# Where the two causal masks of a tile stand beside the scans, and the order of TensorE's two products

## The chip, the cores and the metric

The kernel runs on one core of one Trainium2 chip. The metric is the device time of one execution in microseconds (us). TensorE (PE, with its weight loads as PEld), VectorE (DVE), ScalarE (ACT), GpSimd (POOL) and the DMA queues work side by side, each through its own instructions in program order, and wait for one another only through semaphores.

## The reference, cut to what matters

```python
# attention: B, H, S, D = 4, 8, 768, 48; state is D x D for each head
for t in range(S):
    state = alpha[:, :, t, :, None] * state + k_t (outer) v_t
    y[:, :, t] = q_t @ state
# y as [3072, 384] tokens, then
x = gate_w * (relu(x @ w1[e]) @ w2[e])      # the expert e with the largest logit, 8 experts, 1024 wide
out = square(relu(x @ w_in)) @ w_out        # 2048 wide
```

The recurrence is computed in chunks of 128 steps. With a chunk's running product of alpha folded into q (qt) and the running product from the other end into k (kt), the output of a chunk is a masked product (qt by kt, causal, times v) plus a cross product (qt times the state at the chunk's start), and the state moves on by kt times v.

## The kernel before, in words

There are 24 tiles of 128 tokens, six to a sequence. The attention takes roughly the first 154 us; expert layers and the last feed-forward layer follow.

`prep(n)` is VectorE's work for a tile, five instructions: the forward scan `acum` (L460), a small reciprocal, the backward scan `rs` (L464), and the two products `qt` (L466) and `kt` (L468). `qk_mm(n)` multiplies kt by qt on TensorE into two PSUM tiles `sp` (L488, j = 0 and 1), ScalarE copies each to SBUF (L491), and GpSimd's `affine_select` (L477) sets what lies above the diagonal to zero; the result is `pm`. `k_T(n)` transposes kt (L499) and ScalarE copies it (L501). `kv_mm(n)` forms the new state in PSUM (L511, L515) and VectorE writes it as `sd` (L518). `y_mm(n)` gathers in one PSUM tile `y` the masked product (L529) and, where the tile is not the first of its sequence, the cross product with the state (L532); ScalarE copies it out (L534).

The order on every engine is that of the code. Step n of the main loop issues `qk_mm(n + 1)`, `k_T(n + 1)`, `kv_mm(n)`, `prep(n + 3)`, `y_mm(n)`, and between them the gate: `gate_lg` (L208, L216), `gate_a` to `gate_s`, and `ts()`, which transposes a finished tile of y (xtr, L283), scales it on ScalarE (xb, L287) and stores it (xs, L291). From step 16 on, the loop also loads and splits the first expert's weights (L543, L544), and in step 21 GpSimd gathers the first tokens by indirect DMA (`gather(0)`, L608), for which all early stores of xs must have landed.

A mask is tied to VectorE by a wait: `marks[n, 1]` is VectorE's last instruction before the forward scan of tile n, `marks[n, 0]` the reciprocal after it. Mask j = 0 of tile n + 1 is issued in `qk_mm(n + 1)` with the mark of the reciprocal of prep(n + 2), which VectorE has then usually passed; mask j = 1 is issued after prep(n + 3) with the mark ahead of that prep's forward scan. The copies go to `pa` (2 buffers), the masks write `pm` (4 buffers).

Of the kernel before, what the change touches and what calls it, by code (L numbers as in the profile page):

```python
# [11 lines left out]
F32 = mybir.dt.float32  # L12
# [6 lines left out]
ALU = mybir.AluOpType  # L19
# [3 lines left out]
ET = mybir.EngineType  # L23
# [4 lines left out]
C = 128  # L28
# [29 lines left out]
def body(ctx, tc, qka, v, alpha, mod, wg, mbias, w1, w2, w_in, w_out, out):  # L58
# [395 lines left out]
    def prep(n):  # L454
# [3 lines left out]
        acum = at2.tile([RP, NP, CA], F32, tag="acum", name="acum", bufs=3)  # L458
        marks[n, 1] = next((i for i in reversed(nc.cur_bb.bb.instructions) if i.engine == ET.DVE), None)
        V.tensor_tensor_scan(acum.rearrange("p a c -> p (a c)"), al, one0.rearrange("p a c -> p (a c)"), 0.0, op0=ALU.mult, op1=ALU.max)  # L460
        rz = raz[n % NR]
        marks[n, 0] = V.reciprocal(rz[:, :, C + 1], acum[:, :, C]).ins
        rs = at2.tile([RP, NP, CA], F32, tag="rs", name="rs", bufs=1)
# [7 lines left out]

    preps, pms, kTs, sds, xts, yts = {}, {}, {}, {}, {}, {}
    pas = {}

    def mask(n, j, mark):
        pmt = at2.tile([128, 4, C], F32, tag="pm", name="pm", bufs=4)
        m = G.affine_select(out=pmt, in_=pas.pop((n, j)), pattern=[[0, 4], [1, C]], compare_op=ALU.is_ge, fill=0.0, base=0, channel_multiplier=-1)  # L477
        if mark in marks:
            tc.add_manual_dep(m.ins, marks[mark].name, mybir.DependencyInfo(mybir.DependencyClass.Sync, mybir.DependencyReason.DATA), reason="beside a scan")
        pms.setdefault(n, []).append(pmt)  # L480

    def qk_mm(n):
        pr = preps[n]
        sps = [ps_a.tile([128, 4, C], F32, tag="sp", name="sp", bufs=2) for _ in range(2)]
        for p in range(NP):
            for j, sp in enumerate(sps):
                rows = slice(64 * j, 64 * j + D)
                PE.matmul(sp[:, p, :], pr["kt"][rows, p, :], pr["qt"][rows, p, :], start=True, stop=True)  # L488
        for j, sp in enumerate(sps):
            pas[n, j] = at2.tile([128, 4, C], F32, tag="pa", name="pa")  # L490
            A.copy(pas[n, j], sp)  # L491
        mask(n, 0, (n + 1, 0))

# [10 lines left out]
    def kv_mm(n):  # L504
# [14 lines left out]
        sds[n + 1] = sd  # L519

    def y_mm(n):
        vv, pm, pr = vs.pop(n), pms.pop(n), preps[n]
        y = ps_a.tile([128, 2, 512], F32, tag="y", name="y")
        cross = n % NCH > 0
        v2 = vv.rearrange("s h d -> s (h d)")
        quads = [(p, j, HEAD[p][j] % 2, p // 2, (64, D)[HEAD[p][j] % 2]) for p in range(NP) for j in range(2)]
        for p, j, c, b, w in quads:
            h = HEAD[p][j]
            PE.matmul(y[64 * c:64 * c + w, j, b * C:(b + 1) * C], v2[:, h * D:h * D + w], pm[j][:, p, :], start=(b == 0), stop=(b == 1 and not cross))  # L529
        if cross:  # L530
            for p, j, c, b, w in quads:
                PE.matmul(y[64 * c:64 * c + w, j, b * C:(b + 1) * C], sds[n][64 * j:64 * j + D, p * D:p * D + w], pr["qt"][64 * j:64 * j + D, p, :], start=False, stop=(b == 1))  # L532
        x = gt.tile([RP, NP, C], F32, tag="yt", name="yt", bufs=12)
        A.copy(x.rearrange("r (j b) c -> r j (b c)", j=2), y[:RP, :, :2 * C])  # L534
        yts[n] = x
# [189 lines left out]
    qk_mm(0)  # L725
    mask(0, 1, None)
    k_T(0)
# [24 lines left out]
    for n in range(N):  # L752
# [5 lines left out]
        if n + 1 < N:  # L758
            qk_mm(n + 1)
            k_T(n + 1)  # L760
        ts()
# [6 lines left out]
        if n + 1 < N:  # L768
            mask(n + 1, 1, (n + 3, 1))
        do(n, "mid")  # L770
# [496 lines left out]
```

## Time and profile before

| | us |
|---|---|
| median of 3 runs (lowest to highest) | 799.75 (799.49 to 800.62) |
| the profiled execution: its time | 800.67 |
| its span | 798.5 |
| TensorE busy in the span | 757.9 |
| VectorE busy | 489.1 |
| ScalarE busy | 324.3 |
| GpSimd busy | 190.4 |

The span is one profiled execution from its first to its last instruction; the time is taken around it. Busy time is a sum over stages that have different limits, so the argument is made stage by stage.

### The profile page before, as it was taken

To read this page: it belongs to the slowest core of one execution; us is meant where nothing else is said; L and a number is where in the kernel's file an instruction comes from. 1 tells how busy PE (TensorE), PEld (TensorE's weight loads), DVE (VectorE), ACT (ScalarE), POOL (GpSimd) and SP (SyncE) were. 2 spreads that over 40 slices of the span, in tenths; PEclk is the share of its full clock that TensorE was granted. 3 is DMA by queue.
4 is the path that set the end of the run, shared out by engine and by line. 5 is a ranking of instruction groups with operands and counts; after the bars stand their busy time and mean duration, and the time that the engine had idled before them with its cause. 6 is when DMAs were issued, how large, how long until landed. Compare 5 with 4: busy or idle time off the path is not lost.

```text
span 798.5 us, 13142 instructions
## 1 busy us (share of the span) xinstructions
PE 757.9 (95%) x5167; PEld 664.8 (83%) x5167; DVE 489.1 (61%) x811; ACT 324.3 (41%) x582; POOL 190.4 (24%) x178
## 2 busy tenths in 40 slices
PE   6987977799999999999999999999999999999995
PEld 5776866689878888889889999999999999999985
DVE  6999997577788788697873444544544343343340
ACT  2444545535444534445553432333342333233240
POOL 5564532104463554342200010010000001002001
PEclk9998999999999999999999999999999999999998
DMA  8674966247987688669530040021000001000001
GB/s 222 175 208 144 253 182 216 71 147 193 229 142 280 227 189 266 153 232 190 148 120 1 0 145 1 1 83 63 1 21 21 1 0 40 1 1 30 10 1 43
DMA packets 42558, 88.80 MB, mean 111 GB/s; under 512 B 11149, under 2 KB 26535, under 8 KB 42487
## 3 DMA queue, kind: packets, MB, share of 16 engines
q1 hardware_dynamic: 39287, 78.04, 35.1%
q0 software_dynamic: 3200, 9.83, 3.8%
q8 instruction: 42, 0.69, 0.4%
q14 instruction: 29, 0.24, 0.1%
HBM read 72.10 MB, written 15.76 MB: 110 GB/s over the span
## 4 chain that ended last, share of the span: by engine, by line
PE 78%; DVE 13%; DMA 3%; issue 2%; ACT 2%; POOL 0%; SPq 0%; POOLq 0%; DVEq 0%; ACTq 0%
PE acc L635 8%; PE acc L633 8%; PE acc L634 8%; PE h L634 8%; PE h L635 8%; PE h L633 8%; PE oo L633 4%; PE oo L634 4%; PE oo L635 4%; PE hps L633 4%; PE hps L634 4%; PE hps L635 4%; DVE rs L464 2%; DVE acum L460 2%; PE sp L488 2%
## 5 line engine op out<-in xcount | busy, mean ns | idle before, releaser
L991 DVE TENSOR_TENSOR r<-r 128x512 f32<-128x512 f32 x96 | 68.7, 716 | 143.9 <-ACT r L990 143.8
L635 PE MATMUL acc<-w2h,hl 128*128 128x384 f32 x372 | 125.7, 338 | 0.3 <-DVE hl L544 0.2
L633 PE MATMUL acc<-w2h,hh 128*128 128x384 f32 x372 | 125.3, 337 | 0.6 <-ACT hh L543 0.6
L634 PE MATMUL acc<-w2l,hh 128*128 128x384 f32 x372 | 124.9, 336 | 0.0
L990 ACT ACTIVATE r<-h 128x512 f32<-128x512 f32 x96 | 57.4, 598 | 155.1 <-PE h L635 153.7
L635 PE MATMUL h<-xh,w1l 128*128 128x512 f32 x288 | 113.9, 395 | 0.0
L634 PE MATMUL h<-xl,w1h 128*128 128x512 f32 x288 | 113.6, 395 | 0.0
L633 PE MATMUL h<-xh,w1h 128*128 128x512 f32 x288 | 112.1, 389 | 0.0
L1014 POOL DMA_INDIRECT out_dram<-ob,pidx x24 | 23.4, 974 | 366.7 <-ACT ob L1012 325.6
L544 DVE TENSOR_TENSOR hl<-r,hh 128x512 fp32r<-128x512 f32 x93 | 64.5, 693 | 63.8 <-PE acc L635 37.0
L543 ACT CAST hh<-r 128x512 fp32r<-128x512 f32 x93 | 57.7, 620 | 80.4 <-DVE r L991 80.4
L633 PEld LDWEIGHTS acc<-w2h,hh 128*128 128x128 f32 x372 | 69.9, 188 | 5.1 <-ACT hh L543 1.0
L477 POOL TENSOR_SCALAR_AFFINE_SELECT pm<-pa 128x512 f32<-128x512 f32 x48 | 58.1, 1214 | 65.3 <-DVE sd L518 30.4
L634 PEld LDWEIGHTS acc<-w2l,hh 128*128 128x128 f32 x372 | 69.8, 188 | 3.8
L635 PEld LDWEIGHTS acc<-w2h,hl 128*128 128x128 f32 x372 | 69.8, 188 | 0.9 <-DVE hl L544 0.9
L633 PE MATMUL hps<-xh,w1h 128*128 128x512 f32 (+1 forms) x192 | 68.0, 354 | 1.2 <-ACT xb L287 0.7
L633 PE MATMUL oo<-hh,w2h 128*128 128x512 f32 (+1 forms) x192 | 68.8, 358 | 0.0
L634 PE MATMUL hps<-xl,w1h 128*128 128x512 f32 (+1 forms) x192 | 67.2, 350 | 0.3 <-DVE xl L544 0.3
L635 PE MATMUL oo<-hh,w2l 128*128 128x512 f32 (+1 forms) x192 | 67.3, 350 | 0.0
L634 PE MATMUL oo<-hl,w2h 128*128 128x512 f32 (+1 forms) x192 | 67.1, 350 | 0.0
L635 PE MATMUL hps<-xh,w1l 128*128 128x512 f32 (+1 forms) x192 | 67.1, 349 | 0.0
L635 PEld LDWEIGHTS h<-xh,w1l 128*128 128x128 f32 x288 | 54.0, 187 | 11.5
(218 smaller groups left out, 1340.0 us busy)
## 6 DMA issues: line engine op xcount, KB each, us to landing
qk<-qka_dram SPq DMA_DIRECT2D x23, 675.5 KB, 5.5
raw<-w_dram SPq DMA_DIRECT2D x21, 512.0 KB, 6.6
raw<-w_dram SPq DMA_DIRECT2D x28, 384.0 KB, 3.8
cvr<-w_in_dram SPq DMA_DIRECT2D x12, 512.0 KB, 6.3
cvr<-w_out_dram SPq DMA_DIRECT2D x12, 512.0 KB, 11.0
vv<-v_dram SPq DMA_DIRECT2D x24, 192.0 KB, 5.7
xs<-xb SPq DMA_DIRECT2D x24, 192.0 KB, 3.4
alr<-alpha_dram SPq DMA_DIRECT2D x9, 512.0 KB, 3.4
```

The lines of the kernel that those rows point to most:

```text
L460: V.tensor_tensor_scan(acum.rearrange("p a c -> p (a c)"), al, one0.rearrange("p a c -> p (a c)"), 0.0, op0=ALU.mult, op1=ALU.max)
L464: V.tensor_tensor_scan(rs.rearrange("p a c -> p (a c)")[:, ::-1], al[:, ::-1], rz.rearrange("p a c -> p (a c)")[:, ::-1], 0.0, op0=ALU.mul ...
L477: m = G.affine_select(out=pmt, in_=pas.pop((n, j)), pattern=[[0, 4], [1, C]], compare_op=ALU.is_ge, fill=0.0, base=0, channel_multiplier=-1)
L488: PE.matmul(sp[:, p, :], pr["kt"][rows, p, :], pr["qt"][rows, p, :], start=True, stop=True)
L543: A.copy(hi, raw)
L544: V.tensor_sub(lo, raw, hi)
L633: PE.matmul(o, ah, bh, start=start, stop=False)
L634: PE.matmul(o, ah, bl, start=False, stop=False)
L635: PE.matmul(o, al, bh, start=False, stop=stop)
L990: A.activation(r, o, AF.Relu)
L991: V.tensor_mul(r, r, r)
L1014: G.indirect_dma_start(out=out, out_offset=bass.IndirectOffsetOnAxis(ap=pidx[:, n:n + 1], axis=0), in_=ob, in_offset=None)
```

## The change: what it does

The mark indices trade places: `marks[n, 0]` is now what precedes the forward scan, `marks[n, 1]` the reciprocal ahead of the backward scan. Both masks of tile n + 1 are issued after prep(n + 3); j = 0 waits for the mark of that prep's forward scan, j = 1 for that of its backward scan. ScalarE copies into `pm` itself, of which there are six, and the mask works in place. The cross product of `y_mm` becomes a function of its own, `y_cross(n)`, issued right behind `qk_mm(n + 1)`; the masked product stays where `y_mm(n)` was and is now the one that ends the accumulation.

```diff
--- before.py
+++ after.py
@@ -456,10 +456,10 @@
         qq, kk = (qk[:, i * NP * C:(i + 1) * NP * C].rearrange("p (a c) -> p a c", c=C) for i in range(2))
         al = qk[:, 2 * NP * C:]
         acum = at2.tile([RP, NP, CA], F32, tag="acum", name="acum", bufs=3)
-        marks[n, 1] = next((i for i in reversed(nc.cur_bb.bb.instructions) if i.engine == ET.DVE), None)
+        marks[n, 0] = next((i for i in reversed(nc.cur_bb.bb.instructions) if i.engine == ET.DVE), None)
         V.tensor_tensor_scan(acum.rearrange("p a c -> p (a c)"), al, one0.rearrange("p a c -> p (a c)"), 0.0, op0=ALU.mult, op1=ALU.max)
         rz = raz[n % NR]
-        marks[n, 0] = V.reciprocal(rz[:, :, C + 1], acum[:, :, C]).ins
+        marks[n, 1] = V.reciprocal(rz[:, :, C + 1], acum[:, :, C]).ins
         rs = at2.tile([RP, NP, CA], F32, tag="rs", name="rs", bufs=1)
         V.tensor_tensor_scan(rs.rearrange("p a c -> p (a c)")[:, ::-1], al[:, ::-1], rz.rearrange("p a c -> p (a c)")[:, ::-1], 0.0, op0=ALU.mult, op1=ALU.add)
         qt = xp.tile([RP, NP, C], F32, tag="xl", name="qt", bufs=4)
@@ -469,15 +469,12 @@
         ae = acum[:, :, C:C + 1]
         return dict(ae=ae, qt=qt, kt=kt)
 
-    preps, pms, kTs, sds, xts, yts = {}, {}, {}, {}, {}, {}
-    pas = {}
-
-    def mask(n, j, mark):
-        pmt = at2.tile([128, 4, C], F32, tag="pm", name="pm", bufs=4)
-        m = G.affine_select(out=pmt, in_=pas.pop((n, j)), pattern=[[0, 4], [1, C]], compare_op=ALU.is_ge, fill=0.0, base=0, channel_multiplier=-1)
-        if mark in marks:
-            tc.add_manual_dep(m.ins, marks[mark].name, mybir.DependencyInfo(mybir.DependencyClass.Sync, mybir.DependencyReason.DATA), reason="beside a scan")
-        pms.setdefault(n, []).append(pmt)
+    preps, pms, kTs, sds, xts, yts, ys = {}, {}, {}, {}, {}, {}, {}
+    def mask(n, j):
+        pm = pms[n][j]
+        m = G.affine_select(out=pm, in_=pm, pattern=[[0, 4], [1, C]], compare_op=ALU.is_ge, fill=0.0, base=0, channel_multiplier=-1)
+        if (n + 2, j) in marks:
+            tc.add_manual_dep(m.ins, marks[n + 2, j].name, mybir.DependencyInfo(mybir.DependencyClass.Sync, mybir.DependencyReason.DATA), reason="beside a scan")
 
     def qk_mm(n):
         pr = preps[n]
@@ -486,10 +483,10 @@
             for j, sp in enumerate(sps):
                 rows = slice(64 * j, 64 * j + D)
                 PE.matmul(sp[:, p, :], pr["kt"][rows, p, :], pr["qt"][rows, p, :], start=True, stop=True)
-        for j, sp in enumerate(sps):
-            pas[n, j] = at2.tile([128, 4, C], F32, tag="pa", name="pa")
-            A.copy(pas[n, j], sp)
-        mask(n, 0, (n + 1, 0))
+        for sp in sps:
+            pm = at2.tile([128, 4, C], F32, tag="pm", name="pm", bufs=6)
+            A.copy(pm, sp)
+            pms.setdefault(n, []).append(pm)
 
     def k_T(n):
         if n % NCH == NCH - 1:
@@ -518,18 +515,21 @@
         V.tensor_tensor(sd[:, :NP * D].rearrange("r (p d) -> r p d", d=D), kv, preps[n]["ae"].to_broadcast(shp), op=ALU.mult)
         sds[n + 1] = sd
 
+    quads = [(p, j, HEAD[p][j] % 2, p // 2, (64, D)[HEAD[p][j] % 2]) for p in range(NP) for j in range(2)]
+
+    def y_cross(n):
+        ys[n] = ps_a.tile([128, 2, 512], F32, tag="y", name="y")
+        if n % NCH > 0:
+            for p, j, c, b, w in quads:
+                PE.matmul(ys[n][64 * c:64 * c + w, j, b * C:(b + 1) * C], sds[n][64 * j:64 * j + D, p * D:p * D + w], preps[n]["qt"][64 * j:64 * j + D, p, :], start=(b == 0), stop=False)
+
     def y_mm(n):
-        vv, pm, pr = vs.pop(n), pms.pop(n), preps[n]
-        y = ps_a.tile([128, 2, 512], F32, tag="y", name="y")
-        cross = n % NCH > 0
+        vv, pm, y = vs.pop(n), pms.pop(n), ys.pop(n)
+        first = n % NCH == 0
         v2 = vv.rearrange("s h d -> s (h d)")
-        quads = [(p, j, HEAD[p][j] % 2, p // 2, (64, D)[HEAD[p][j] % 2]) for p in range(NP) for j in range(2)]
         for p, j, c, b, w in quads:
             h = HEAD[p][j]
-            PE.matmul(y[64 * c:64 * c + w, j, b * C:(b + 1) * C], v2[:, h * D:h * D + w], pm[j][:, p, :], start=(b == 0), stop=(b == 1 and not cross))
-        if cross:
-            for p, j, c, b, w in quads:
-                PE.matmul(y[64 * c:64 * c + w, j, b * C:(b + 1) * C], sds[n][64 * j:64 * j + D, p * D:p * D + w], pr["qt"][64 * j:64 * j + D, p, :], start=False, stop=(b == 1))
+            PE.matmul(y[64 * c:64 * c + w, j, b * C:(b + 1) * C], v2[:, h * D:h * D + w], pm[j][:, p, :], start=(first and b == 0), stop=(b == 1))
         x = gt.tile([RP, NP, C], F32, tag="yt", name="yt", bufs=12)
         A.copy(x.rearrange("r (j b) c -> r j (b c)", j=2), y[:RP, :, :2 * C])
         yts[n] = x
@@ -723,7 +723,8 @@
 
     preps[0] = prep(0)
     qk_mm(0)
-    mask(0, 1, None)
+    mask(0, 0)
+    mask(0, 1)
     k_T(0)
     loaded[3] = load(3)
     preps[1] = prep(1)
@@ -757,6 +758,8 @@
         do(n, "pre")
         if n + 1 < N:
             qk_mm(n + 1)
+        y_cross(n)
+        if n + 1 < N:
             k_T(n + 1)
         ts()
         do(n, "kv")
@@ -766,7 +769,8 @@
         if n + 3 < N:
             preps[n + 3] = prep(n + 3)
         if n + 1 < N:
-            mask(n + 1, 1, (n + 3, 1))
+            mask(n + 1, 0)
+            mask(n + 1, 1)
         do(n, "mid")
         if n > GROUPS[EG + 1][0] + 3:
             pop(2)
```

TensorE in step 2 (sp is `qk_mm` of tile 3, kp the transposes of `k_T`, kv the state, y the output). Before, the end of one step and the beginning of the next:

```order
L515 MATMUL kv<-vv,kT 64x48
L515 MATMUL kv<-vv,kT 48x48
L529 MATMUL y<-pm,vv 48x128
L529 MATMUL y<-pm,vv 64x128 x2
L529 MATMUL y<-pm,vv 48x128 x2
L529 MATMUL y<-pm,vv 64x128 x2
L529 MATMUL y<-pm,vv 48x128
L532 MATMUL y<-qt,sd_122 48x128
L532 MATMUL y<-qt,sd_122 64x128 x2
L532 MATMUL y<-qt,sd_122 48x128 x2
L532 MATMUL y<-qt,sd_122 64x128 x2
L532 MATMUL y<-qt,sd_122 48x128
```

After the change, from the beginning of step 2 (the lines have moved: L485 is `qk_mm`, L524 the cross product, L496 the transposes, L508 and L512 the state):

```order
L485 MATMUL sp<-qt,kt 128x128 x8
L524 MATMUL y<-qt,sd_123 48x128
L524 MATMUL y<-qt,sd_123 64x128 x2
L524 MATMUL y<-qt,sd_123 48x128 x2
L524 MATMUL y<-qt,sd_123 64x128 x2
L524 MATMUL y<-qt,sd_123 48x128
L496 MATMUL kp<-ident,kt 128x112 x4
L508 MATMUL kv<-sd_123,ident 112x192
L512 MATMUL kv<-vv,kT 64x48
```

The cross product has moved from the end of the step to the place between `qk_mm` and `k_T`, so it is now ahead of the state product of the same step.

GpSimd from the end of the set-up to the second gather, with what each waits for (xg is the gather). Before:

```order
L183 MEMSET oh_all 128x200
L477 AFFINE_SELECT pm<-pa 128x512 [waits DVE_49,Activation_49] x43
L608 DMA xg<-xs,ids_e 128x384 [waits DMAHW4_49,DMAHW5_49,DMAHW3_49,DMAHW7_49,DMAHW0_49,DVE_49]
L608 DMA xg<-xs,ids_e 128x384
L477 AFFINE_SELECT pm<-pa 128x512 [waits Activation_49] x3
```

After:

```order
L183 MEMSET oh_all 128x200
L475 AFFINE_SELECT pm<-pm 128x512 [waits DVE_49,Activation_49] x42
L608 DMA xg<-xs,ids_e 128x384 [waits DMAHW4_49,DMAHW5_49,DMAHW3_49,DMAHW7_49,DMAHW0_49,DVE_49]
L608 DMA xg<-xs,ids_e 128x384
L475 AFFINE_SELECT pm<-pm 128x512 [waits Activation_49] x4
```

One mask, j = 0 of tile 22, has moved from the front of the gather to its back.

## Rows read from the trace of the kernel before

**Rows 1.** Busy time of each engine in three stretches, with granted clock (PEclk)

```profile
20.00:64.00 44.00, 38.94 (x676) 31.77 (x675) 42.19 (x65) 20.00 (x39) 23.54 (x19) 1.00 0.69 190
64.00:91.00 27.00, 24.30 (x356) 20.29 (x353) 24.42 (x48) 15.04 (x35) 12.27 (x10) 0.87 0.62 183
...
133.40:154.00 20.60, 15.78 (x191) 12.56 (x191) 11.18 (x31) 9.10 (x21) 3.94 (x5) 0.83 0.33 100
```

**Rows 2.** Timeline of one prep on VectorE, with its masks: start, us, engine, operation

```profile
39.14 1.22 DVE L460 TENSOR_TENSOR_SCAN acum<-qk,one 112x520 f32<-112x520 f32 x1
39.34 1.45 POOL L477 TENSOR_SCALAR_AFFINE_SELECT pm<-pa 128x512 f32<-128x512 f32 x1 [1.54 <-DVE sd L518]
...
40.61 1.27 DVE L464 TENSOR_TENSOR_SCAN rs<-qk,raz 112x520 f32<-112x520 f32 x1
...
40.96 1.35 POOL L477 TENSOR_SCALAR_AFFINE_SELECT pm<-pa 128x512 f32<-128x512 f32 x1 [0.17 <-ACT pa L491]
...
41.80 1.05 DVE L466 TENSOR_TENSOR qt<-qk,acum 112x512 f32<-112x512 f32 x1
...
42.78 0.68 DVE L468 TENSOR_TENSOR kt<-qk,rs 112x512 f32<-112x512 f32 x1
43.38 1.23 DVE L460 TENSOR_TENSOR_SCAN acum<-qk,one 112x520 f32<-112x520 f32 x1
```

**Rows 3.** Timeline: two masks back to back, and the prep beside them

```profile
52.74 3.10 POOL L477 TENSOR_SCALAR_AFFINE_SELECT pm<-pa 128x512 f32<-128x512 f32 x2 [1.54 <-DVE sd L518]
...
55.33 1.05 DVE L466 TENSOR_TENSOR qt<-qk,acum 112x512 f32<-112x512 f32 x1
```

**Rows 4.** Timeline: a prep whose qt meets no mask

```profile
89.03 0.66 DVE L466 TENSOR_TENSOR qt<-qk,acum 112x512 f32<-112x512 f32 x1
...
89.61 0.68 DVE L468 TENSOR_TENSOR kt<-qk,rs 112x512 f32<-112x512 f32 x1
```

**Rows 5.** All of qt by line: count and shortest, median, longest ns

```profile
L466 DVE TENSOR_TENSOR qt<-qk,acum x24: 658/1048/1056, 6.4 to 128.1; 112x512 f32<-112x512 f32 x24
```

**Rows 6.** Timeline of TensorE in one step of that stretch

```profile
47.85 1.16 PE L488 MATMUL sp<-qt,kt 48*128 48x128 f32 x16 [1.07 <-DVE kt L468]
...
51.29 0.66 PE L532 MATMUL y<-qt,sd 48*48 48x128 f32 x16
```

**Rows 7.** Timeline: VectorE's sd where it waits for the state product

```profile
23.67 0.36 DVE L518 TENSOR_TENSOR sd<-kv,acum 112x192 f32<-112x192 f32 x1 [0.59 <-POOL pm L477]
...
90.51 0.36 DVE L518 TENSOR_TENSOR sd<-kv,acum 112x192 f32<-112x192 f32 x1 [0.23 <-PE kv L515]
```

**Rows 8.** Timeline: TensorE's wait for ScalarE in step 19

```profile
116.58 0.60 PE L283 MATMUL xtr<-ident,yt 112*128 112x112 f32 x4 [1.36 <-ACT xb L287]
```

**Rows 9.** Timeline: behind the last prep

```profile
129.87 0.66 POOL L477 TENSOR_SCALAR_AFFINE_SELECT pm<-pa 128x512 f32<-128x512 f32 x1 [2.74 <-ACT pa L491]
130.06 0.51 DVE L318 TENSOR_TENSOR e_aeb<-e_ae,e_ef 128x32 f16<-128x32 f32 x1
```

**Rows 10.** Timeline: from the gather to the last masked product

```profile
141.02 1.96 POOL L477 TENSOR_SCALAR_AFFINE_SELECT pm<-pa 128x512 f32<-128x512 f32 x3
141.70 0.58 ACT L491 COPY pa<-sp 128x512 f32<-128x512 f32 x1 [1.16 <-POOL pm L477]
142.58 1.09 PE L529 MATMUL y<-pm,vv 128*48 128x128 f32 x16
143.17 1.83 DVE L544 TENSOR_TENSOR w2l<-raw,w2h 128x768 fp32r<-128x768 f32 x2 [0.60 <-ACT w2h L543]
147.52 0.63 PE L283 MATMUL xtr<-ident,yt 112*128 112x112 f32 x4 [2.72 <-ACT xb L287]
149.36 1.98 PE L529 MATMUL y<-pm,vv 128*48 128x128 f32 x16
```

**Rows 11.** Chain that ended last, its pieces in order of time: start, us, what

```profile
90.91 1.25 DVE acum L460
...
151.34 0.63 PE y L532 x14
```

## The prediction

> **What bounds the kernel now.** I read the stretches first, because the change touches only the attention, about 154 of 798.5 us; what it gives or takes there is carried to the end, since behind it the chain of waits goes on through compute. In the stretch 20 to 64 us [rows 1] VectorE is busy 42.19 of 44.00 us and TensorE 38.94: VectorE bounds. From 64 to 91 us TensorE takes over (24.30 of 27.00 at a mean clock of 0.87), and the chain comes back to VectorE at 90.91 [rows 11]. From about 112 to 125 TensorE and ScalarE wait for each other in turn (1.36 us before the row of [rows 8]). From 133.4 to 154 everything has air (15.78 us of 20.60 on the fullest engine [rows 1]): the chain runs over a store, the gather, VectorE and TensorE.
>
> The second view is the timeline of one prep where VectorE bounds [rows 2]. Without sd it runs from 39.14 to 43.38, 4.24 us: scan 1.47 to the next scan's start, 1.19 for that, 0.98 for qt, 0.60 for kt. The reader should see what the two masks do there. The mask issued 0.20 us into the forward scan is over at 40.79, 0.43 us behind that scan's end at 40.36: the reciprocal's gap takes it. The mask issued 0.35 us into the backward scan is over at 42.31, again 0.43 us behind that scan's end at 41.88, and in the place of a gap there stands qt, whose length is 1.05 us. Where no mask meets it, qt has 0.66 us and the next instruction starts 0.58 us behind its start instead of 0.98 [rows 2, 4]. A mask beside a scan thus does not run beside it; it comes out behind it, and behind the backward scan that costs 0.98 - 0.58 = 0.40 us.
>
> **The masks, part by part.** After the change every mask of tiles 1 to 21 stands as this pair does: j = 0 released at the forward scan, j = 1 at the reciprocal. That order is already in the trace: two masks back to back from 52.74 to 55.84, the first beside the forward and the second beside the backward scan, and qt at 55.33 has its 1.05 us [rows 3]. Could j = 1 slip in ahead of the backward scan? Its release comes at the reciprocal's end, but j = 0 is over only at 40.79, behind the scan's start at 40.61 [rows 2], so it is queued behind j = 0 and comes too late. The 0.40 stays where it is today: the median qt of all 24 is 1.05 us already [rows 5], three more preps lose the same on kt. Term for the VectorE-bound stretches: **0**. Bounds: if the second mask vanished from VectorE's path, -0.40 in each of the some 14 preps that lose it and bound (-5.6); if it cost more than today, the far end is the whole mask alone, 0.66 [rows 9], in place of 0.40: +0.26 in each, +3.6. I take 0 since the rows show this very order.
>
> Five preps that today have neither qt nor kt delayed get the 0.40 as well. Three of them stand where VectorE waits anyway; the two others are counted below.
>
> The Trainium skill (SBUF — State Buffer, section "SBUF: two separate sides") says that VectorE with two SBUF inputs and GpSimd take a shared port pair as an exclusive lock for a whole instruction, and that the loser fully blocks. The trace agrees that the mask does not get through during a scan; by the rule to the letter qt would be held for a whole mask, 0.66 us, where the rows show 0.40, and the sum below would be 0.5 us higher for the two new delays on the path.
>
> **The masked product's new wait.** Mask j = 1 now ends one prep later. In a VectorE-bound step kt ends at a time T, TensorE starts `qk_mm` 0.2 us later, and sd, forward scan, backward scan, 0.5 us of qt bring the mask's end at about T + 0.38 + 1.47 + 1.19 + 0.51 = T + 3.55. TensorE's step takes 47.85 to 51.95, 4.10 us [rows 6]; with the cross product early, the masked product could start at about T + 3.2 and now starts at T + 3.65 and ends near T + 4.75, against the next kt at T + 4.62 with its 0.2 us: it just fits. Behind it in TensorE's queue stands the next `qk_mm`, and the state product behind that is needed one step later, with about a microsecond to spare. Cost: **0**; the cover is that microsecond, and without it what TensorE loses would pass to sd.
>
> **The cross product ahead of the state product.** It takes 0.66 us [rows 6] and now delays kv, so sd, wherever VectorE waits for kv. In step 1, sd at 23.67 had been waiting 0.59 us (the row names the mask as releaser, but the state product ended just there) [rows 7], and from then on VectorE bounds: **+0.66**; VectorE's own new delay of 0.40 in that prep hides in the 0.59. In steps 13 and 14 sd waits for kv too, in step 14 for 0.23 us [rows 7]. The first moves by 0.66; the prep behind it also gets the new 0.40, less the 0.23 of wait, so sd at 90.51 moves by 0.66 + 0.40 - 0.23 = **+0.83**, more than the state product's own delay. From 90.91 on the chain is VectorE's [rows 11]. TensorE's work as a whole is the same, so what lies between is not paid twice. Bounds: 0 (if kv is not what sd waits for) and twice 0.83.
>
> **112.6 to 125.** TensorE waits 1.36 us for ScalarE, whose queue is two copies of sp, kT, then xb [rows 8]. The cross product fills part of the wait, but it also pushes kp and thus kT back, since one cross product (0.66 [rows 6]) now stands between `qk_mm` and kp; by my count along the two queues the end of step 19 comes 0.3 us earlier, and step 20 loses nearly all of it by the later kT. Term: **-0.05**; bounds -1.3 (all of both) and +0.3.
>
> **125 to the gather.** The last prep gets 0.40, on the path. In return the mask at 129.87 no longer stands beside e_aeb, which has 0.51 us for a tile of 32 columns [rows 9]; I estimate that 0.3 comes back. Term: **+0.10**, bounds 0 and 0.40.
>
> **From the gather to the experts.** Four masks now follow the gather instead of three; three take 1.96 us [rows 10], so the two that the masked product of tile 22 needs end at 141.02 + 1.31 = 142.33, and that product started at 142.58: covered, by 0.25. ScalarE no longer waits 1.16 us for a mask to free `pa` [rows 10], since six buffers stand ready, so the cast w2h comes earlier and VectorE need not wait 0.60 for it; the chain from there is w2l, the gate, xb, and xtr at 147.52 [rows 10]. The earlier cross products of tiles 21 and 22 also bring the gate's logits forward by about 0.3. But w2l then meets the last two masks. Term: **-0.70**, bounds 0 and -1.0. Last, the cross product of tile 23, 0.63 us at 151.34 [rows 11], moves into the 2.72 us in which TensorE waits before 147.52 [rows 10]: **-0.63**, bounds 0 and, if TensorE's clock then stays up, another -0.9 (the masked product at 149.36 has 1.98 us, the like one at 142.58 1.09 [rows 10]).
>
> **The sum.** 0 + 0 + 0.66 + 0.83 - 0.05 + 0.10 - 0.70 - 0.63 = +0.2 us on 800.67, the profiled execution's time. That one lies 0.92 above the median of the runs, so I put the change on the median: 799.75 + 0.2, about **800.0**. A change below 0.2% (1.6 us) can't be told from none.
>
> **The rivals.** *The masks do hide.* If j = 1 let qt go, VectorE's step would fall by 0.40 to 3.84 + 0.38 for sd, and TensorE's 4.10 plus 0.2 would bound at 4.3 against 4.62: 14 steps by 0.3 is 4.2, so about 795.8. For it: the change puts both masks at the beginnings of scans, and one more row without contention would do. Against it: the pair [rows 3], and 1.05 in rows where the mask was 0.35 us into the scan [rows 2]. Chance 0.08.
>
> *The back end gains more.* The clock stays up at 149, w2l gains its whole 1.0, and the 1.36 us waits give back half a microsecond each: 800.0 - 0.9 - 0.3 - 0.95 = 797.9. For it: the mean clock there is 0.83 [rows 1], and the cross product shortens the idle time in front. Against it: some 2 us of that idle time remain. Chance 0.20.
>
> *A lower clock earlier (slower).* The masked product's new wait makes an idle piece on TensorE in the middle of each step. If the granted clock fell to its lower level (1.2 of 2.4 GHz) once more in a stretch where TensorE bounds, the price is what it is in 64 to 91 today: 0.13 of 27.00 us, 3.5 us, so about 803.5. It decides when that wait, 0.45 us by the sum above, grows with others to the 2 to 3 us in front of today's falls. For it: from 64 to 91 TensorE has no reserve. Against it: the clock is 1.00 all through 20 to 64 [rows 1] with an idle piece of about that size in each step. Chance 0.14.
>
> *The gather's masks decide (slower).* If masks beside w2l need 1.35 to 1.45 us each [rows 2] instead of 0.65, the masked product of tile 22 is 1.3 late, the -0.70 is gone, and the time is about 802.0. Chance 0.10.
>
> The forecast has the remaining 0.48. From these cases: faster by over 0.2% (below 798.1) 0.26, slower (above 801.4) 0.24, in between 0.50. The range that holds 8 in 10 reaches from 797.2 to 802.4; the likeliest case alone has 798.6 to 801.2.
>
> **What would show it.** Right: qt 1.05 us in nearly all preps; the period in 24 to 63 us unchanged at about 4.6; the forward scan that follows sd at 23.67 some 0.6 later; no wait of ScalarE for `pm`; experts' first product near 154. Wrong: qt at 0.66 in the VectorE-bound steps, a clock below 1.00 in 20 to 64, or waits of VectorE's sd for kv that come back in each step.

## The result, and the profile after

The change made the kernel slower. In the comparison of the two kernels the median rose from 798.91 us (11 runs, 796.93 to 801.62) to 804.14 us (11 runs, 800.83 to 807.53): ratio 1.0061, 95% interval 1.0038 to 1.0083. The prediction was 800.0 us, with 802.4 as its upper end.

The profiled execution took 805.73 us, its span is 803.6. The first view is the one of [rows 1]: busy time by engine in the same three stretches, with granted clock in the third column from the end.

```profile
20.00:64.00 44.00, 39.76 (x684) 31.80 (x684) 42.76 (x66) 19.93 (x40) 27.18 (x19) 1.00 0.69 192
64.00:91.00 27.00, 24.35 (x356) 20.11 (x350) 24.20 (x45) 15.42 (x35) 13.79 (x10) 0.87 0.61 179
133.40:154.00 20.60, 14.87 (x160) 11.44 (x159) 11.33 (x30) 7.11 (x15) 4.48 (x6) 0.70 0.32 96
```

The VectorE-bound stretch looks as it did, and so does 64 to 91; the last one has a clock of 0.70 where it had 0.83. The step on VectorE that answers to [rows 2]:

```profile
38.23 1.22 DVE L460 TENSOR_TENSOR_SCAN acum<-qk,one 112x520 f32<-112x520 f32 x1
38.43 2.97 POOL L475 TENSOR_SCALAR_AFFINE_SELECT pm<-pm 128x512 f32<-128x512 f32 x2 [1.54 <-DVE sd L515]
...
39.70 1.27 DVE L464 TENSOR_TENSOR_SCAN rs<-qk,raz 112x520 f32<-112x520 f32 x1
40.90 1.05 DVE L466 TENSOR_TENSOR qt<-qk,acum 112x512 f32<-112x512 f32 x1
41.87 0.68 DVE L468 TENSOR_TENSOR kt<-qk,rs 112x512 f32<-112x512 f32 x1
42.47 1.23 DVE L460 TENSOR_TENSOR_SCAN acum<-qk,one 112x520 f32<-112x520 f32 x1
```

From scan to scan it is 4.24 us again, and qt has its 1.05 us. The two masks stand back to back beside the scans and come out behind them, as in [rows 3].

The attention as a whole ends later. Behind the gather, where [rows 10] stood:

```profile
139.58 1.92 PE L208 MATMUL gps<-yt,wg_sb 112*32 112x128 f32 x8
...
141.43 1.32 PE L485 MATMUL sp<-qt,kt 48*128 48x128 f32 x16
142.67 0.66 PE L524 MATMUL y<-qt,sd 48*48 48x128 f32 x16
...
143.26 0.24 PE L216 MATMUL gps<-ident,ls 32*128 32x32 f32 x1
...
143.78 2.39 POOL L475 TENSOR_SCALAR_AFFINE_SELECT pm<-pm 128x512 f32<-128x512 f32 x4
...
144.24 0.20 DVE L224 TENSOR_TENSOR L<-gps,lbias 128x40 f32<-128x40 f32 x1 [3.91 <-PE gps L216]
144.47 0.20 DVE L226 TENSOR_REDUCE mx<-L 128x5 f32<-128x40 f32 x1
144.70 0.95 DVE L228 TENSOR_TENSOR dl<-L,mx 128x40 f32<-128x40 f32 x1
...
145.69 0.55 DVE L230 SCALAR_TENSOR_TENSOR sc<-dl,edesc 128x40 f32<-128x40 f32 x1
...
146.50 0.20 DVE L233 TENSOR_TENSOR oh_all<-sc,sm 128x40 bf16<-128x40 f32 x1
...
146.75 0.18 PE L240 MATMUL gps<-oh_all,lt_b 128*128 128x48 bf16 x1 [2.14 <-DVE oh_all L233]
...
146.88 1.82 DVE L544 TENSOR_TENSOR w2l<-raw,w2h 128x768 fp32r<-128x768 f32 x2
146.97 1.09 PE L532 MATMUL y<-pm,vv 128*48 128x128 f32 x16
...
151.69 1.01 PE L283 MATMUL xtr<-ident,yt 112*128 112x112 f32 x4 [0.87 <-ACT xb L287]
...
157.76 0.39 PE L633 MATMUL hps<-xh,w1h 128*128 128x256 f32 x1 [0.73 <-ACT xb L287]
```

The same piece before the change:

```profile
138.50 1.16 PE L488 MATMUL sp<-qt,kt 48*128 48x128 f32 x16
...
139.59 0.24 PE L216 MATMUL gps<-ident,ls 32*128 32x32 f32 x1
...
139.98 0.20 DVE L224 TENSOR_TENSOR L<-gps,lbias 128x40 f32<-128x40 f32 x1 [2.96 <-PE gps L216]
...
140.44 0.65 DVE L228 TENSOR_TENSOR dl<-L,mx 128x40 f32<-128x40 f32 x1
...
141.99 0.32 DVE L233 TENSOR_TENSOR oh_all<-sc,sm 128x40 bf16<-128x40 f32 x1
```

The reader is to see two things. The gate's small product L216 starts 1.83 us after `qk_mm`, since the cross product of tile 22 now stands between them (before, 1.09 us; but the cross product of tile 21 has left the place ahead of `qk_mm`, so this alone doesn't make L216 late). And the gate's dl and sc, tiles of 40 columns, take 0.95 and 0.55 us beside the masks, where the reduction mx ahead of them takes 0.20. Only when oh_all is done can TensorE go on (it waited 2.14 us). w2l, which waited in [rows 10], doesn't any more. The last row is the experts' first product, at 157.76 us.

**One profile isn't enough.** Both kernels were profiled three times in all. In the following table every number is a difference between the starts of two rows of one profile: two forward scans (L460) of VectorE, or the last forward scan and the experts' first product (hps). The last column is TensorE's mean granted clock between these two. The four columns of stretches hold what comes at about 66 to 88, 88 to 109, 109 to 124 and 124 to 156 us. The names that begin with r are further profiles of before and after. Three kernels are explained below: e1 has the masks' part of the change alone, e12 the same with the old places from tile 19 on; e11 has all masks at their old places.

| profile | span | prep 13 to 17 | 17 to 21 | 21 to 23 | 23 to experts | experts start | clock, 23 to experts |
|---|---|---|---|---|---|---|---|
| before | 798.5 | 21.31 | 21.08 | 13.47 | 28.48 | 153.94 | 0.88 |
| r_before | 796.9 | 19.98 | 21.05 | 13.46 | 28.70 | 151.49 | 0.82 |
| r2_before | 801.8 | 21.69 | 21.09 | 15.65 | 27.73 | 155.05 | 0.88 |
| e11_buffers_only | 796.5 | 19.98 | 21.09 | 13.47 | 28.16 | 150.88 | 0.88 |
| e1_masks_only | 804.4 | 21.78 | 21.05 | 15.64 | 29.79 | 156.80 | 0.83 |
| e12_old_places_late | 801.1 | 21.78 | 21.49 | 15.65 | 29.60 | 156.60 | 0.83 |
| after | 803.6 | 22.37 | 21.05 | 15.81 | 29.83 | 157.76 | 0.77 |
| r_after | 802.0 | 19.94 | 21.06 | 15.81 | 29.72 | 155.61 | 0.77 |
| r2_after | 799.3 | 22.34 | 21.08 | 13.20 | 29.59 | 153.85 | 0.77 |

The stretch ahead of these (prep 4 to 13) is 45.50 to 45.56 us in every profile of every kernel.

In the first three stretches, where a number changes within one kernel, the granted clock changes with it. Stretch 70 to 80 and 110 to 120 us, of r_before, r_after, after and r2_after in turn:

```profile
70.00:80.00 10.00, 10.00 (x167) 8.37 (x164) 9.86 (x17) 7.44 (x19) 4.27 (x4) 1.00 0.92 265
110.00:120.00 10.00, 8.10 (x110) 6.57 (x110) 9.63 (x21) 6.58 (x16) 4.09 (x4) 1.00 0.82 259
```

```profile
70.00:80.00 10.00, 10.00 (x158) 8.17 (x159) 9.83 (x18) 7.98 (x20) 5.84 (x5) 1.00 0.74 229
110.00:120.00 10.00, 8.48 (x84) 6.92 (x85) 7.45 (x17) 5.03 (x13) 4.20 (x3) 0.66 0.76 222
```

```profile
70.00:80.00 10.00, 10.00 (x108) 8.44 (x109) 8.54 (x16) 5.89 (x14) 4.86 (x4) 0.66 0.59 178
110.00:120.00 10.00, 7.81 (x76) 6.17 (x73) 7.73 (x26) 5.01 (x12) 3.10 (x2) 0.67 0.54 159
```

```profile
70.00:80.00 10.00, 10.00 (x110) 8.13 (x108) 8.59 (x16) 6.03 (x14) 4.44 (x4) 0.69 0.66 194
110.00:120.00 10.00, 7.40 (x110) 6.08 (x114) 9.29 (x24) 6.23 (x16) 5.22 (x4) 1.00 0.66 190
```

A fall to the lower level at about 70 makes prep 13 to 17 longer by 1.3 to 1.8 us in the old order of TensorE and by 2.4 in the new one; a fall at about 112 makes 21 to 23 longer by 2.2 in the old and 2.6 in the new. Neither is fixed by the program: the same kernel has them in one execution and not in another. So the two kernels are compared where the clock has done the same in 13 to 17 and in 21 to 23. With the fall at 70 alone (before, r2_after) these two and the last stretch differ by +1.03, -0.27 and +1.11. With both falls (r2_before, after): +0.68, +0.16 and +2.10. Behind prep 13 that is 1.9 to 2.9 us, where the prediction's sum has -0.45. In the last stretch the clock has not done the same, as the last column shows. The rows of before and after:

```profile
125.46:153.94 28.48, 20.77 (x288) 16.36 (x282) 18.87 (x44) 14.87 (x32) 6.17 (x7) 0.88 0.37 118
```

```profile
127.93:157.76 29.83, 22.44 (x272) 17.61 (x266) 18.99 (x44) 15.00 (x32) 7.57 (x8) 0.77 0.27 83
```

So a part of the third number can be the clock's. The executions differ in more than this: prep 2 starts at 12.3 to 14.4 us, whatever the kernel.

### The profile page after: what moved, and what is told of

Its sections match the earlier page's. It is cut to its first block, busy times and chain, and to the rows that moved or that the text cites. A ratio compares the mean times of both kernels' runs of the same rounds, so it can differ in the third digit from the quotient of the medians.

```text
span 803.6 us, 13162 instructions
## 1 busy us (share of the span) xinstructions
PE 764.7 (95%) x5167; PEld 669.2 (83%) x5167; DVE 489.5 (61%) x811; ACT 325.5 (40%) x582; POOL 199.8 (25%) x178
## 4 chain that ended last, share of the span: by engine, by line
PE 72%; DVE 4%; DMA 2%; issue 1%; ACT 1%; SPq 0%; POOL 0%; POOLq 0%; DVEq 0%; ACTq 0%
PE acc L635 8%; PE acc L633 8%; PE acc L634 8%; PE h L634 8%; PE h L635 8%; PE h L633 8%; PE oo L633 4%; PE oo L634 4%; PE oo L635 4%; PE hps L633 4%; PE hps L634 4%; PE hps L635 4%; DMA cvr<-w_in_dram 1%; DVE w2l L544 1%; PE xt L626 1%
## 5 line engine op out<-in xcount | busy, mean ns | idle before, releaser
L475 POOL TENSOR_SCALAR_AFFINE_SELECT pm<-pm 128x512 f32<-128x512 f32 x48 | 68.1, 1442 | 56.2 <-DVE sd L515 43.2
```

The source lines that it names most:

```text
L475: m = G.affine_select(out=pm, in_=pm, pattern=[[0, 4], [1, C]], compare_op=ALU.is_ge, fill=0.0, base=0, channel_multiplier=-1)
```

## The experiments

What costs? Three theories were tried. The masks' wait on TensorE or the cross product brings on falls of the clock where TensorE bounds; or the masks behind the gather hold up the gate; or the cross product ahead of the state product delays what VectorE waits for.

The time of before differs a little from one set of runs to another (medians 798.91 to 801.45), so each kernel is told by its ratio to before in its own set. What is left out of a kernel's computation is said where it is.

**The parts alone.** First the masks (places, marks, six buffers) with TensorE's order as it was; this is the diff of the change without `y_cross`.

> The masks, their marks and the six buffers as after the change; TensorE's order as before (state product, masked product, cross product last). Theory A (TensorE's clock falls once more in the attention and stays low longer, because the cross product has left the end of the step; the masks alone cost nothing): no extra fall at 114 us, the sum of low clock as before (mean about 0.986), 799 to 800 us. Rival B (the masks' new place is what costs, since the masked product waits for them and TensorE's pauses grow): about 803 to 805 us, clock 0.973 to 0.978, like the changed kernel.

Measured: 805.69 us, ratio 1.0046 (1.0030 to 1.0061). Second, the cross product alone.

```diff
             qk_mm(n + 1)
+        y_cross(n)
```

> The kernel before with one part of the change alone: the cross product directly behind the product of q and k; masks, marks and buffers as before. Theory A (the cross product's place makes the clock fall): about 803 to 805 us with a clock of 0.973 to 0.978 and a low clock around 114 to 121 us. Rival B (the masks make it): 799 us, clock 0.986; VectorE's state instruction then waits for TensorE in steps 13, 14 and 19 as far as the cross product stands ahead of it, at most 1 us in all.

Measured: 802.6 us, ratio 1.0018 (1.0001 to 1.0036). In its profile 13 to 17 is 19.98 (no fall at 70), 21 to 23 is 15.74 (a fall at 112), and 23 to experts 27.37, shorter than in any profile of the table. Third, the change with the cross product directly ahead of the masked product, so that it doesn't delay the state product.

```diff
-        y_cross(n)
...
+        y_cross(n)
         y_mm(n)
```

> The changed kernel with the cross product moved behind the state product, directly ahead of the masked product. It takes away the cross product's delay of the state product, and keeps the masks. If that delay (0.5 us near 86 us, up to 2.4 us near 120) is what the change costs: 800 to 801 us. If the clock falls because of the masks' wait or of pauses that stay: 803 to 805 us with the clock below 0.98.

Measured: 805.86 us, ratio 1.0055 (1.0033 to 1.0077). It follows that the masks carry most of the loss and the place of the cross product little (0.18%, with an interval that begins just above zero). In e3's profile prep 13 to 17 is 21.84, as with the masks alone: the 0.5 us that it lies below the 22.37 of after is the cross product.

**Filled pauses.** If low clock is what costs, products that nobody reads, put into the pauses in front of the falls, should bring the time back. Unread products of 112 columns (112x128 by 112x112) were added at five places.

```diff
+    def fill(k):
+        kp = ps_a.tile([128, NP, RP], F32, tag="kp", name="fill")
+        for _ in range(k):
+            PE.matmul(kp[:, 0, :], one0[:, 0, :128], one0[:, 0, :RP], start=True, stop=True)
```

> The changed kernel with small products that nobody reads, put on TensorE in five of its pauses (near 105, 111, 132, 134 and 145 us), each set no longer than the pause. If the lower clock behind those pauses is what costs: the clock stays at 1.00 from 100 to 155 us, the mean rises to about 0.99 and the time falls by 3 to 5 us to about 799 to 801. If the clock is a side effect: the time stays at 803 to 805 us whatever the clock does.

Measured: 815.15 us, ratio 1.0171 (1.0155 to 1.0187). The clock was 1.00 from 80 to 160, but the products (20, 20, 6, 28 and 28 of them) were longer than the pauses and delayed the chain: the experts started at 163.58. Then with 6, 5, 3, 8 and 8, and the like in the kernel before:

> The changed kernel with unread products in five of TensorE's pauses, as in the run before but fewer (3 to 8 in a pause, at the 0.24 us each that they were seen to take, so that they end inside it). Theory A (TensorE's lower clock from 107 to 122 and from 135 to 155 us is what the change costs): clock 1.00 from 100 to 155 us, VectorE's 22nd forward scan 2 us earlier, the experts' first product 3 to 4 us earlier, the time 3 to 4 us below the changed kernel's, at the level of the kernel before. Rival B (VectorE's new delays and waits cost, and the clock follows them): the clock is up, and the time stays 4 to 5 us above the kernel before.

> The kernel before with the same unread products in its own pauses between 104 and 148 us. Theory A: its low clock from 107 to 111, 134 to 138 and 147 to 152 us goes too; only the last two lie on the chain (the store and gather hide one of them), so 1 to 2 us faster than the kernel before. Rival B: no change in time.

Measured: after with fills 804.76 us, ratio 1.0051 (1.0035 to 1.0066); before with fills 804.72 us, ratio 1.0044 (1.0030 to 1.0058). The late falls were gone (clock 1.00 from 130 to 150 in both), the one at 110 to 120 was not (0.68 and 0.66). In the kernel before, the two early sets cost: its ratio is 1.0044 with them and, below, 1.0007 without; in after they make no difference. With the late ones alone, in after and in before:

> The changed kernel with unread products in the three late pauses alone (near 132, 134 and 145 us), none near 105 and 111. The run with all five had the clock at 1.00 from 130 to 150 and came 2.3 us earlier from the last prep to the experts, and lost that between the scans of preps 21 and 23. Theory A: from the last prep to the experts 27.5 us instead of 29.8, the stretch 21 to 23 as in the changed kernel (15.8), the time 2 us below the changed kernel's. Rival B: no change in time.

> The kernel before with unread products in the three late pauses and in the one near 147 us alone. Theory A: from the last prep to the experts 27 us instead of 28.5, all else as before: 1.5 us faster than the kernel before, which would beat both. Rival B: no change.

Measured: 805.1 us, ratio 1.0050 (1.0030 to 1.0070), and 801.9 us, ratio 1.0007 (0.9994 to 1.0020). In after the stretch from prep 23 to the experts went down to 26.82 us in that profile (clock 1.00 from 80 to 150), but what follows it took 649.0 us there, against 645.4 to 646.4 in after. And in a second profile of the same kernel (below) the clock fell again at 147, its mean over the stretch was 0.83, and the stretch took 30.49. The medians didn't move: in these runs the clock bought with extra products doesn't shorten the kernel.

**The gather behind the masks.** The gather of the first tokens moved behind the masks of tile 22, so that these are done before the gate's dl and sc.

```diff
-                    at(n + 5, "pool", lambda: (early.pop()(), gather(0)))
+                    at(n + 5, "pool", lambda: early.pop()())
+                    at(n + 5, "mid", lambda: gather(0))
```

> The changed kernel with one thing moved: the first gather is issued on GpSimd behind both masks of tile 22 instead of ahead of them, so two masks follow it, not four. Theory C (part of the cost is that four masks right behind the gather stand against the gate's small VectorE instructions): from the gate's first instruction L to oh_all 1.2 to 1.6 us instead of 2.3 to 2.7, the experts start about 1 us earlier behind the last prep, the time 1 us below the changed kernel's. Rival (only the clock costs): those intervals and the time as in the changed kernel.

Measured: 805.47 us (801.28 to 812.17), ratio 1.0061 (1.0035 to 1.0086). From L to oh_all it takes 1.38 us in place of 2.26, and 23 to experts is 28.90 in place of 29.8, with the clock's mean at 0.76; the time didn't follow. (Two masks, those of tile 23, are still there: dl takes 0.41.)

**No wait for the masks.** The masked product reads the masked buffers of the tile before, so that its output within a chunk is another tile's and TensorE has no mask to wait for.

```diff
-        vv, pm, y = vs.pop(n), pms.pop(n), ys.pop(n)
+        vv, pm, y = vs.pop(n), pms[max(n - 1, 0)], ys.pop(n)
```

> The changed kernel, but the masked product of a tile reads the masked buffers of the tile before it, which are ready a step earlier, so TensorE never waits for a mask; all masks, copies and their places are the same (the part of the output within a chunk is that of another tile). If the masked product's wait makes TensorE's pauses, and with them the low clock from 107 to 122: that stretch is at 1.00 and the time 2 to 3 us below the changed kernel's. If the masks cost through VectorE and GpSimd: the time as in the changed kernel.

Measured: 804.82 us (5 runs), ratio 1.0039 (1.0026 to 1.0052), prep 4 to 13 45.53, 13 to 17 22.38 with the fall at 70, 21 to 23 13.20 without one at 112, and 23 to experts 31.20 at a mean clock of 0.73. Without the wait the fall at 70 is there all the same, and most of the loss stays.

**Profiles of the two kernels once more.**

> The kernel before once more, for its profile. If falls of TensorE's clock are a matter of each execution: the stretches of low clock lie elsewhere than in the first profile, or have another length, and the experts' first product moves by as much. If they are fixed by the program: the same three stretches (64 to 91, 105 to 112, 133 to 154 us) and the experts at 153 to 154 us.

> The changed kernel once more, for its profile. If falls of the clock are a matter of each execution: low stretches elsewhere than 107 to 122 and 135 to 155 us, and another start of the experts than 157.8 us. If the program fixes them: the same.

> The kernel before, profiled once more. Theory A (the attention's end alone sets the time): the experts' first product lies at 151.5 to 154, and from it to the last product oo it takes 231.4 to 231.7 us as in the two profiles so far. Theory B (the token gathers of the second round of tiles land late in some executions of any kernel): that stretch is sometimes 233 to 235 us, with a wait of TensorE for xg of 0.7 to 1.3 us in it.

> The changed kernel, profiled once more. Theory A: the experts' first product at 155.6 to 157.8, the stretch behind it 232.0 to 232.3, the clock below 1.00 in 110 to 120. Theory B: the same beginning, but the stretch behind it anywhere from 232 to 235 us.

Measured: 799.04, 804.23, 803.86 and 801.52 us, one execution each; the last two stand the other way round than the medians. Their stretches are in the table above. From the experts' first product to the last product oo of the experts it took 231.4 and 231.7 us in the first two profiles of before, 232.3 and 232.0 in those of after, 234.9 in e7 and 235.7 in e8. So these two were profiled again as well:

> The changed kernel with the first gather behind the masks, profiled once more. If the longer stretch from the experts' first product to the last oo (234.9 us, with 1.0 us of waits for xg) belongs to this order, it is 234.5 to 235.2 again; if it belongs to the execution, it lies anywhere between 231.5 and 235. The experts' first product lies at 153.7 if the clock stays at 1.00 in 110 to 120, at 156 if not.

> The changed kernel with unread products at 132, 134 and 145 us, profiled once more. If the stretch of 235.2 us behind the experts' first product belongs to these products, it is 235 again, with a wait for xg of about 1.2 us; if it belongs to the execution, it lies anywhere between 231.5 and 235.

Measured: 802.83 and 809.83 us. That stretch took 232.7 us in r2_before and 231.7 in r2_after, with no wait for xg above 0.03, 232.7 in the second profile of e7 and 235.2 in that of e8. From the experts' first product to the end of the span e7's kernel took 649.0 us in its first profile and 646.7 in its second, e8's 649.0 and 648.7; before took 644.6, 645.4 and 646.8, after 645.8, 646.4 and 645.4. In the stretch 150 to 240 us TensorE's waits (line, releaser, us in total, times, longest) show for e7 and then for its second profile:

```profile
PE xt L626 <- DMA xg<-xs,ids: 1.0, 2, 0.8
```

```profile
PE xt L626 <- DMA xg<-xs,ids: 0.2, 1, 0.2
```

The gathered tokens of the second round of tiles land later in some executions. That is a part of what differs behind the attention, not all of it, and not a property of the order in e7. In e8 it is there both times (waits for xg of 1.2 and 2.1 us in all), so there it may belong to the added products. For before and after these rests have nearly the same mean, 645.6 and 645.9: what these profiles differ by in the mean lies in the attention, where the experts start 2.2 us later (153.5 and 155.7).

**Which piece of the masks.** Two kernels split e1. The first keeps every mask at its old place and mark, and has only the copies into six buffers and the masking in place.

```diff
-            pas[n, j] = at2.tile([128, 4, C], F32, tag="pa", name="pa")
-            A.copy(pas[n, j], sp)
+            pm = at2.tile([128, 4, C], F32, tag="pm", name="pm", bufs=6)
+            A.copy(pm, sp)
+            pms.setdefault(n, []).append(pm)
```

> The kernel before with the copies going straight into six buffers and the masks in place, but every mask at the place and with the mark that it had, and TensorE's order as before. Theory A (the masks' new place behind the gather costs the 4.4 us that the masks alone cost): as before, ratio 0.999 to 1.001, from the last forward scan to the experts' first product 27.7 to 28.7 us. Theory B (the buffers or the masking in place cost): ratio 1.003 to 1.006.

Measured: 800.32 us (12 runs), ratio 0.9998 (0.9978 to 1.0017), 28.16 us from the last forward scan to the experts. The second is e1 with the old places from tile 19 on.

```diff
+        if n >= 19:
+            mask(n, 0, (n + 1, 1))
...
-            mask(n + 1, 0)
-            mask(n + 1, 1)
+            if n + 1 < 19:
+                mask(n + 1, 0, (n + 3, 0))
+            mask(n + 1, 1, (n + 3, 1 if n + 1 < 19 else 0))
```

> The masks alone (TensorE's order as before, six buffers, in place), with the new places for tiles 1 to 18 and the old ones from tile 19 on, so that three masks and not four follow the gather. Theory A: as before, ratio 0.999 to 1.001, 27.7 to 28.7 us from the last forward scan to the experts' first product. Theory C (the new places ahead of 110 us cost, through the later masked product): ratio 1.003 to 1.006 although the end of the attention is as before.

Measured: 804.08 us (9 runs), ratio 1.0037 (1.0020 to 1.0053). So buffers and masking in place cost nothing that can be told from noise, and the new places of tiles 1 to 18 alone cost nearly what the masks as a whole do (1.0046). The theory that the fourth mask behind the gather is the cost falls: e12 has three there, and its 23 to experts is still 29.60. Its masks met dl all the same:

```profile
142.80 1.80 POOL L475 TENSOR_SCALAR_AFFINE_SELECT pm<-pm 128x512 f32<-128x512 f32 x3
...
143.18 1.49 DVE L228 TENSOR_TENSOR dl<-L,mx 128x40 f32<-128x40 f32 x1
```

What the new places do to TensorE is seen in its waits from 20 to 76 us, in before, in e12 and then in after:

```profile
PE y L529 <- POOL pm L477: 0.3, 1, 0.3
```

```profile
PE y L529 <- POOL pm L475: 3.6, 8, 1.1
```

```profile
PE y L532 <- POOL pm L475: 1.7, 2, 1.1
```

## Why the prediction was wrong

**Right.** The masks in the VectorE-bound stretches, **0**: qt is 1.05 us, the step 4.24 and the stretch of nine preps 45.5 us in every kernel, so *The masks do hide* is out. ScalarE waits for no buffer, and w2l for no cast. "125 to the gather" **+0.10**: from the last forward scan to the first split weight w1l it takes 5.10 us in all three profiles of after and 5.03 in those of before, +0.07; to the gather itself it is +0.1 in the mean.

**"The cross product ahead of the state product".** **+0.66** in step 1 failed: from prep 2 to 4 it takes 9.41, 10.19 and 9.82 us in the profiles of after against 9.71, 9.34 and 9.41, which differ with the execution. The wait of 0.59 at 23.67 [rows 7] wasn't the program's; in after sd at 22.82 waits for nothing, in r_after 0.69, in r_before 0.22. **+0.83** was of the right size where the clock falls at 70 (+0.7 to +1.0; the 0.5 of e3 is its share for the cross product alone) and nothing where it doesn't (19.94 against 19.98). It took a fall of the clock for a fixed part of the kernel.

**"112.6 to 125" -0.05.** Like with like it is -0.27 without the fall and +0.16 with it, so the term was good. But the +2.2 to 2.6 of the fall itself was in none of the term's bounds, since the one profile read beforehand had none there. Profiles with the masks' old places have it in 4 of 7 and those with the new ones in 6 of 13, so it isn't the change's doing.

**"From the gather to the experts" -0.70 and -0.63.** This is the step that failed, with the wrong sign: 27.7 to 28.7 us before, 29.6 to 29.8 after, +1.4 in the mean where -1.3 was forecast. Both waits did go, as predicted. And two gains were there where the rest let them be seen. With the clock at 1.00 from 130 to 150 us (the runs with unread products) L216 starts 12.65 us behind the last forward scan in e8 and 12.99 in e9 (the scan is L467 there), so the logits do come 0.3 earlier, as I wrote:

```profile
126.15 1.24 DVE L467 TENSOR_TENSOR_SCAN acum<-qk,one 112x520 f32<-112x520 f32 x1
...
138.80 0.24 PE L216 MATMUL gps<-ident,ls 32*128 32x32 f32 x1
```

```profile
126.94 1.24 DVE L467 TENSOR_TENSOR_SCAN acum<-qk,one 112x520 f32<-112x520 f32 x1
...
139.93 0.24 PE L216 MATMUL gps<-ident,ls 32*128 32x32 f32 x1
```

And the cross product's move alone (e2, masks at their old places) has 27.37 us, against 27.7 to 28.5 in before, r2_before and e11 at the same mean clock, 0.88.

What the sum doesn't have is two things that hold up the gate. From the last forward scan to oh_all it takes 18.57, 18.42 and 18.46 us in the profiles of after and 16.53, 16.81 and 17.84 in those of before: +1.4 in the mean, as much as the whole stretch.

The first is the masks beside dl and sc: from L to oh_all 2.26, 2.70 and 2.20 us against 2.01, 1.54 and 1.91, **+0.6** in the mean; e1, the masks alone, has 2.79, and e2, the cross product alone, 1.29. e7 shows their price: with two masks instead of four behind the gather it has 1.38 and, in its second profile, 1.32, and 28.90 and 28.99 from prep 23 to the experts, **0.8** less than after at nearly the same mean clock (0.76 and 0.77). I had looked at the masks beside w2l, a long operation behind the gate, and not at the small ones on the chain ahead of it. The Trainium skill (SBUF — State Buffer, section "SBUF: two separate sides") has VectorE operations with two SBUF inputs shut out for as long as GpSimd holds the shared ports. The rows agree: dl and sc, with two inputs, are held, and mx, with one, keeps its 0.20 us beside the same masks. For qt the measured 0.40 holds as before. The rival *The gather's masks decide* had the stretch and about the price (802.0), with w2l as a wrong mechanism.

The second is a lower clock. In after, L216 starts at 15.2 to 15.4 us behind the last forward scan, in before at 14.1, 15.0 and 15.4. The place of the cross product isn't what makes it late: e1 and e12, where nothing stands between `qk_mm` and L216 (1.09 us), have 15.5 and 15.4. The gate's L208 just ahead of `qk_mm` takes 1.92 us in all three profiles of after, 1.24, 1.34 and 1.71 in those of before, 1.06 in e9 at a clock of 1.00. Over the whole stretch the mean clock is 0.77 in all three of after and 0.88, 0.82 and 0.88 in before. How much of the +1.4 is the clock's stays open; in e8's two profiles, one program, the stretch took 26.82 us at 1.00 and 30.49 at 0.83.

**What remains is a lower clock.** The rival *A lower clock earlier* gave 803.5 and chance 0.14, for one more fall where TensorE bounds; it priced that at 3.5 us, where a fall cost 1.3 to 2.6. What the runs show for it: the mean granted clock is 0.9755 over the 11 runs of after (0.973 to 0.983) and 0.9815 over 29 runs of before (0.976 to 0.986); e1 has 0.977, e12 0.978, e11 0.981. And the fall at 70 to 80 is there in 12 of 13 profiles of kernels with the masks' new places, in 3 of 7 of those with the old ones (a fourth, e6, has 0.83 there, which makes 13 to 17 0.2 longer). My estimate from this is 12/13 of 2.4 less 3/7 of 1.6, about +1.5 us for 13 to 17. With +1.4 from prep 23 on that gives some 2.9 of the 5.2 us between the medians, close to the lower end of their interval (0.38% of 799 is 3.0). The mean clock says little by itself: r_after has 0.972, the lowest of the six profiles of before and after, and its span is 1.6 us below that of after. Where VectorE bounds, a low clock shows no price: r_after and e11 have 0.83 in 60 to 70 us and 45.52 and 45.56 us from prep 4 to 13, as all others.

What that rival had as its cause isn't shown. It blamed "the masked product's new wait"; e10 has no such wait and still has the fall. The pause just in front of it, 2.7 us for xb, is there in r_before too, where the clock stays up. The five profiles without this fall all have a lower clock at 10 to 20 us instead, but so do six with it; and three of the five (r_after, e11, e2) have a shorter fall just ahead of it, in 60 to 70, where it costs nothing. Why the masks of tiles 1 to 18 make the fall likelier, though no stretch before it is longer by their doing, stays open, as does what is left of the 5.2 us: the three profiles of each kernel differ by 2.6 us in their mean span, half of what the medians do.

## What to carry to other kernels

Before an order is judged by one profile, take several of the same program: here a fall of the clock of 1.3 to 2.6 us came and went between executions, and in these profiles one of them came more often with the masks' new places (12 of 13 against 3 of 7). Check moved masks against the small operations on the chain and not only the long ones: dl, 0.20 us alone, took 0.9 to 1.4. When a product is pulled ahead on an engine, count what has left the queue ahead of a row as well as what now stands there, and time the row from a fixed point (here the last forward scan) before its new neighbour is blamed. Clock bought with extra products has to be paid on the same engine; here it never came back.

## What was unexpected in the hardware

The clock at its lower level is seen in TensorE's rows themselves. `qk_mm` and the cross product right behind the pause at 70, in after and then in r_after:

```profile
69.98 1.99 PE L485 MATMUL sp<-qt,kt 48*128 48x128 f32 x16
71.90 1.12 PE L524 MATMUL y<-qt,sd 48*48 48x128 f32 x16
```

```profile
70.35 1.16 PE L485 MATMUL sp<-qt,kt 48*128 48x128 f32 x16
71.45 0.66 PE L524 MATMUL y<-qt,sd 48*48 48x128 f32 x16
```

The same program, the same work: in one execution at 1.2 GHz, in the other at 2.4. The subtraction dl of 128x40 took 0.20 us in r_before, and 0.95, 1.39 and 0.89 us beside the masks in the three profiles of after, 1.66 in e3: it differs with when the two meet. In the other two profiles of before it took 0.65 and 0.47, the first beside GpSimd's second gather, which ends at 141.01 as dl does at 141.09.
